# One subtraction per attention pass, from VectorE to GpSimd: the low half of expert 0's first weight

## The chip, the cores and the metric

The program runs on one core of a Trainium2 chip. The core has five engines with queues of their own, which meet at semaphores only: PE (TensorE, matmuls; PEld is its weight load), DVE (VectorE), ACT (ScalarE), POOL (GpSimd) and SP (SyncE, which here only issues DMA). The metric is the device time of one execution in microseconds (us).

## What is computed

Attention in two parts over 64 heads (8 batches of 8, 576 positions, 64 columns), added up, and then a mixture of 8 experts in which each of the 4608 tokens goes to one expert:

```python
q_d, k_d, v_d = means over groups of 4 positions      # "pooled"
out_up = np.repeat(sm_attn(q_d, k_d, v_d), 4, axis=2)
mask = np.abs(pos[:, None] - pos[None, :]) < 4        # local attention
out_local = softmax(where(mask, scale * q @ k.T, -1e9)) @ v
x = (out_up + out_local) as [4608, 512]
logits = x @ w_gate; expert_idx = argmax(logits)
for e in range(8):
    h = np.maximum(x_sorted[lo:hi] @ w1[e], 0.0)
    y_sorted[lo:hi] = h @ w2[e]
return gate_w[:, None] * y
```

All data are float32. A float32 product in the expert part is made of three matmuls on halves: each matrix is split into a high half (rounded to the type fp32r) and a low half (the difference), and high x high, high x low and low x high are added.

## The kernel before

**Passes.** The attention loop handles two heads at a time. `steps(i)` issues pass i, for i from 0 to 31, and the table `PASS` sets the order of everything in it. A pass works on several pairs at once: its entry `(f, a)` runs step f for pair i - a. What one engine does in a pass is issued to its queue in that order and runs in that order. Marks such as `"@w1"` are places where further work is put in with `at((pass, mark), ...)`.

**POOL in a pass.** In this order: `pool_v` (vdt, L216) for pair i; `pool_qk` (qkt, L205) for pair i + 1, which adds up the queries and keys in pairs; at the mark `@sc` none, one or two scatters, each of them a one-element memset of `spacer` (L470) and an indirect DMA of 128 rows from the buffer `xr` into the DRAM tensor `xs` (L471); `pool_qk2` (qkd, L211) for pair i + 1; `pool_v2` (vds, L222) for pair i. Of the passes spoken of here, 15, 17, 21, 23, 25 and 29 have two scatters, 18, 19, 22, 26, 27 and 30 have one, 16, 20, 24 and 28 have none.

**The other engines.** PE makes the scores on pooled data, `s_d` (L285, 12 matmuls), from qkd. DVE takes their maximum (mxd, L290), normalises (L274, L271), and in the next pass takes the maximum and sums of the local part (L249, L259), adds the result of an older pair into XT (L364, after ACT's outd, L354) and subtracts (L253). The bank pD that `s_d` writes is the only one, and comes free when ACT's three exponentials of the pair before (L299) and DVE's L271 are done. Passes 15, 19, 23 and 27 have a stage of the routing (`route_b`) on DVE and ACT; passes 16, 20, 24 and 28 have its last stage (`route_c`): among others DVE's L424 to L437 and ACT's L427 and L429. L429 and L437 write token numbers and gates into the rows of `xr` that earlier scatters read, and wait for these DMAs to have landed.

**The split of expert 0's first weight.** `split_w1` makes the halves w1h and w1l of a piece of the raw weight: ACT copies with rounding (L181), another engine subtracts (L182). For expert 0 it is called with `quarters`, one piece of 128x256 at the mark `@w1` of each of passes 15 to 30:

```python
    for j in range(4):
        for q in range(4):
            at((15 + j * 4 + q, "@w1"), split_w1, 0, j, (q,))
```

`@w1` stands behind `max_scale` (ACT, L293) and `norm` (DVE, L271) and ahead of `pool_qk2`, `exp_d` (ACT, L299) and `pool_v2`. For experts 1 to 7 it is called without `quarters`, in the expert part, on pieces of 128x512. The halves of expert 0 are first used behind the last pass.

Of the kernel before, what the change touches and what calls it, by code (L numbers as in the profile page):

```python
# [90 lines left out]
def attention_moe_kernel(ctx: ExitStack, tc: tile.TileContext, qk, vw, vd, wg, w1, w2, cst, csb, out):  # L91
    nc = tc.nc
# [80 lines left out]
    def split_w1(e, k, quarters=None, halves=(0, 1)):  # L173
        if (e, k) not in W1:
            pl = wpool if e % 2 == 0 else wodd[0]
            W1[e, k] = (pl.tile([128, F], F32R, name=f"w1h{k}"), pl.tile([128, F], F32R, name=f"w1l{k}"))
        hi, lo = W1[e, k]
        src = raws[place[1, e, k]]
        for s in [slice(a * 512, (a + 1) * 512) for a in halves] if quarters is None else [
                slice(a * 256, (a + 1) * 256) for a in quarters]:  # L180
            nc.scalar.activation(hi[:, s], src[:, s], AF.Copy)  # L181
            nc.vector.tensor_sub(lo[:, s], src[:, s], hi[:, s])  # L182

    outds = [p2.tile([128, QPAD // 2], F32, name=f"outd{i}", bufs=1) for i in range(2)]

# [602 lines left out]
# [3 lines that stand above are left out]
# [93 lines left out]
    for e in range(E):  # L884
        for f in range(8):
            if e > 0:
                s1(e, f)
                if f == 3:
                    rest = prep(e, 4, hold=True)
                if f == 4:  # L890
                    rest()
                split_w2(e, f)
                if f % 2 == 1:
                    raw_ahead(place[2, e, f // 2] + 6)
            else:
                s1(e, f, slice(EARLY.stop, FIRST))
            if e + 1 < E:
                if f == (0 if e == 0 else 4):
                    x_load(e + 1, 1)
                if f == 0 and e > 0:  # L900
                    x_load(e + 1, 0)
                if f == 4:
                    gi_load(e + 1, 0, 5)
                split_w1(e + 1, f // 2, halves=(f % 2,))
                if f % 2 == 1:
                    raw_ahead(place[1, e + 1, f // 2] + 6)
                if f == 6 and e + 2 < E:
                    pad_after(e + 2)
                if f == 7:
                    prep(e + 1, 0, 1)  # L910
                    gi_make(e + 1, 0, 5)
# [54 lines left out]
```

## Time and profile before

| | |
|---|---|
| median of 3 runs | 669.18 us (665.74 to 670.09) |
| the profiled execution's own time | 662.55 us |
| its span, first to last instruction | 660.6 us |
| PE busy | 625.5 us (95%) |
| DVE busy | 371.9 us (56%) |
| ACT busy | 320.0 us (48%) |
| POOL busy | 216.3 us (33%) |

A share of the whole span mixes three parts: the attention loop up to about 200 us, a stretch up to about 245 us in which the last tokens are routed, scattered and read back, and the experts, which are PE's. The passes that the change touches lie between 100 and 196 us; rows of that stretch are what is read below. In them an engine's row starts some hundredths of a microsecond before the row ahead of it has ended, so what an instruction takes out of its queue is read from start to start.

### The profile page before, as it was taken

How to read it: one execution, taken by the hardware profiler on the slowest of the kernel's cores; microseconds unless marked ns; L12 is line 12 of the kernel's file. 1: busy time of each engine (PE TensorE's matmuls, PEld its weight loads, DVE VectorE, ACT ScalarE, POOL GpSimd, SP SyncE). 2: the span in 40 equal slices, each digit the busy share in tenths (PEclk: the TensorE clock that was granted, in tenths of full speed). 3: DMA queues.
4: the chain of work that ended last, by engine and by line, in shares of the span. 5: the costliest groups of instructions: out<-in, count | busy, mean ns of one | idle time of the engine just before them, and what ended most of it. 6: DMA issues, size and time to landing. Idle time of an engine off the chain costs nothing.

```text
span 660.6 us, 15650 instructions
## 1 busy us (share of the span) xinstructions
PE 625.5 (95%) x6163; PEld 510.3 (77%) x6163; DVE 371.9 (56%) x691; ACT 320.0 (48%) x845; POOL 216.3 (33%) x316
## 2 busy tenths in 40 slices
PE   7988998999998989999999999999999989999994
PEld 3766776777776978888888888888888878888873
DVE  5968899999996646382373065166128247115020
ACT  3656777778785535362362254254236145224120
POOL 6955887888770611101101011101110101110111
PEclk9989999999999989999999999999999999999998
DMA  9999999899534496284176238238228528110001
GB/s 305 286 270 264 291 280 279 261 281 269 170 128 124 150 297 193 63 232 147 52 182 187 66 133 233 65 94 216 99 80 224 178 77 209 48 46 1 33 18 41
DMA packets 66226, 108.52 MB, mean 164 GB/s; under 512 B 15388, under 2 KB 36524, under 8 KB 66112
## 3 DMA queue, kind: packets, MB, share of 16 engines
q1 hardware_dynamic: 59840, 87.62, 47.8%
q0 software_dynamic: 5984, 19.01, 7.9%
q8 instruction: 66, 1.08, 0.7%
q10 hardware_dynamic: 288, 0.42, 0.2%
q14 instruction: 48, 0.39, 0.2%
HBM read 86.98 MB, written 23.67 MB: 167 GB/s over the span
## 4 chain that ended last, share of the span: by engine, by line
PE 68%; issue 10%; DVE 10%; DMA 4%; POOL 3%; ACT 2%; SPq 1%; POOLq 0%; another core or an unknown queue 0%; DVEq 0%; ACTq 0%
PE p L596 8%; PE p L597 8%; PE p L595 8%; PE p L611 7%; PE p L609 7%; PE p L610 7%; PE pD L285 3%; PE pPV L337 2%; PE pX L322 2%; PE pX L691 2%; PE pX L710 2%; DMA vd<-in_vd_dram 2%; PE pPV L350 1%; DVE A L271 1%; PE pS L236 1%
## 5 line engine op out<-in xcount | busy, mean ns | idle before, releaser
L595 PE MATMUL p<-xh,w1h 128*128 128x512 f32 (+1 forms) x288 | 106.7, 370 | 3.2 <-issue 1.9
L616 POOL DMA_INDIRECT out_dram<-y,tix x39 | 38.0, 974 | 212.9 <-ACT y L628 201.5
L596 PE MATMUL p<-xl,w1h 128*128 128x512 f32 (+1 forms) x288 | 106.0, 368 | 0.8 <-DVE xl L543 0.8
L597 PE MATMUL p<-xh,w1l 128*128 128x512 f32 (+1 forms) x288 | 105.9, 368 | 0.0
L609 PE MATMUL p<-w2h,hh 128*128 128x512 f32 x256 | 101.1, 395 | 0.0
L611 PE MATMUL p<-w2h,hl 128*128 128x512 f32 x256 | 99.8, 390 | 0.0
L610 PE MATMUL p<-w2l,hh 128*128 128x512 f32 x256 | 99.6, 389 | 0.0
L600 DVE SCALAR_TENSOR_TENSOR hl<-p,hh 128x512 fp32r<-128x512 f32 (+1 forms) x72 | 45.5, 632 | 93.3 <-ACT hh L599 91.3
L599 ACT ACTIVATE hh<-p 128x512 fp32r<-128x512 f32 (+1 forms) x72 | 39.6, 551 | 78.9 <-PE p L597 78.9
L628 ACT ACTIVATE y<-p,gi 128x512 f32<-128x512 f32 x32 | 22.0, 689 | 93.8 <-PE p L611 89.4
L595 PEld LDWEIGHTS p<-xh,w1h 128*128 128x128 f32 x288 | 55.0, 191 | 13.1 <-issue 2.3
L596 PEld LDWEIGHTS p<-xl,w1h 128*128 128x128 f32 x288 | 55.1, 191 | 9.7 <-DVE xl L543 0.9
L597 PEld LDWEIGHTS p<-xh,w1l 128*128 128x128 f32 x288 | 55.0, 191 | 8.7
L611 PEld LDWEIGHTS p<-w2h,hl 128*128 128x128 f32 x256 | 48.0, 188 | 10.2
L610 PEld LDWEIGHTS p<-w2l,hh 128*128 128x128 f32 x256 | 48.1, 188 | 9.6
L609 PEld LDWEIGHTS p<-w2h,hh 128*128 128x128 f32 x256 | 48.1, 188 | 9.4
L471 POOL DMA_INDIRECT xs<-xr,ix x36 | 36.8, 1021 | 42.0 <-ACT w1h L181 12.4
L182 DVE TENSOR_TENSOR w1l<-raw,w1h 128x512 fp32r<-128x512 f32 (+1 forms) x72 | 49.4, 686 | 0.8
L299 ACT ACTIVATE AD<-pD,mxd 128x144 f32<-128x144 f32 x96 | 35.3, 376 | 19.1 <-DVE A L271 18.8
L543 DVE TENSOR_TENSOR xl<-pX,xh 128x512 fp32r<-128x512 f32 x38 | 24.7, 684 | 35.2 <-ACT xh L542 34.2
L585 DVE TENSOR_TENSOR w2l<-raw,w2h 128x512 fp32r<-128x512 f32 x64 | 43.4, 681 | 1.1 <-ACT w2h L584 0.6
L216 POOL TENSOR_TENSOR vdt<-vd 72x512 f32<-72x512 f32 x32 | 40.8, 1276 | 6.4 <-DMA vd<-in_vd_dram 4.2
(148 smaller groups left out, 1204.7 us busy)
## 6 DMA issues: line engine op xcount, KB each, us to landing
raw<-in_w_dram SPq DMA_DIRECT2D x64, 512.0 KB
qk<-in_qk_dram SPq DMA_DIRECT2D x32, 583.0 KB
vw<-in_vw_dram SPq DMA_DIRECT2D x32, 320.0 KB
vd<-in_vd_dram SPq DMA_DIRECT2D x32, 288.0 KB
xrow<-xs SPq DMA_DIRECT2D x32, 192.0 KB
xrow<-xs SPq DMA_DIRECT2D x32, 128.0 KB
xs<-zs SPq DMA_DIRECT2D x6, 512.0 KB
xs<-pad SPq DMA_DIRECT2D x3, 257.0 KB
```

The costliest lines, as they stand in the source:

```text
L182: nc.vector.tensor_sub(lo[:, s], src[:, s], hi[:, s])
L216: nc.gpsimd.tensor_add(t2, v[:, 0:2], v[:, 2:4])
L585: nc.vector.tensor_sub(lo, src, hi)
L595: nc.tensor.matmul(p, wh[:, fs], xh[:, k, r], start=(k == 0), stop=False)
L596: nc.tensor.matmul(p, wh[:, fs], xl[:, k, r], start=False, stop=False)
L597: nc.tensor.matmul(p, wl[:, fs], xh[:, k, r], start=False, stop=(k == 3))
L599: nc.scalar.activation(hh[:, f, r], p, AF.Relu)
L600: nc.vector.scalar_tensor_tensor(hl[:, f, r], p, 0.0, hh[:, f, r], op0=OP.max, op1=OP.subtract)
L609: nc.tensor.matmul(p, hh, wh, start=(f == 0), stop=False)
L610: nc.tensor.matmul(p, hh, wl, start=False, stop=False)
L611: nc.tensor.matmul(p, hl, wh, start=False, stop=(f == 7))
L616: ins = nc.gpsimd.indirect_dma_start(out=out, out_offset=bass.IndirectOffsetOnAxis(ap=ix, axis=0), in_=y, in_offset=None, bounds_check=N - ...
```

## The change

One line: where `split_w1` is called with `quarters`, that is for expert 0 in the attention loop, the subtraction is issued on POOL instead of DVE. The other calls stay as they are.

```diff
@@ -179,7 +179,7 @@
         for s in [slice(a * 512, (a + 1) * 512) for a in halves] if quarters is None else [
                 slice(a * 256, (a + 1) * 256) for a in quarters]:
             nc.scalar.activation(hi[:, s], src[:, s], AF.Copy)
-            nc.vector.tensor_sub(lo[:, s], src[:, s], hi[:, s])
+            (nc.vector if quarters is None else nc.gpsimd).tensor_sub(lo[:, s], src[:, s], hi[:, s])
```

POOL's queue at passes 15 and 16, with the semaphores that each row waits for (Activation is ACT's, DMAHW and DMASW are DMA queues'); the first two rows are the end of pass 15's second scatter:

```order
 L470 MEMSET spacer 1x1 [waits Pool_49]
 L471 DMA xs<-xr,ix 42112x514 [waits DMASW1_49,Activation_49]
+L182 TENSOR_TENSOR w1l_2008<-raw,w1h_2007 128x256 [waits DMAHW0_49,Activation_49]
 L211 TENSOR_TENSOR qkd<-qkt 128x288 [waits PE_49]
 L222 TENSOR_TENSOR vds<-vdt 72x256
 L216 TENSOR_TENSOR vdt<-vd 72x512 [waits DMAHW0_49,Pool_49]
 L205 TENSOR_TENSOR qkt<-qk 128x576 [waits DMAHW7_49]
+L182 TENSOR_TENSOR w1l_2008<-raw,w1h_2007 128x256 [waits Activation_49]
 L211 TENSOR_TENSOR qkd<-qkt 128x288 [waits PE_49,Pool_49]
```

In each of the sixteen passes the subtraction stands behind the scatters and ahead of qkd, and waits for ACT. POOL's queue at pass 17, with two scatters:

```order
 L205 TENSOR_TENSOR qkt<-qk 128x576 [waits DMAHW2_49]
 L470 MEMSET spacer 1x1
-L471 DMA xs<-xr,ix 42112x514 [waits DMASW2_49,DVE_49,Activation_49]
+L471 DMA xs<-xr,ix 42112x514 [waits DMASW2_49,DVE_49]
 L470 MEMSET spacer 1x1 [waits Pool_49]
 L471 DMA xs<-xr,ix 42112x514 [waits DMASW3_49]
+L182 TENSOR_TENSOR w1l_2008<-raw,w1h_2007 128x256 [waits Activation_49]
 L211 TENSOR_TENSOR qkd<-qkt 128x288 [waits PE_49]
 L222 TENSOR_TENSOR vds<-vdt 72x256
@@ -108,5 +111,6 @@
```

The first scatter no longer waits for ACT itself, since the subtraction of pass 16 ahead of it in the queue has waited for a later instruction of ACT. DVE's queue at the turn from pass 15 to pass 16:

```order
 L274 TENSOR_TENSOR AD<-AD,pD 128x432
 L271 TENSOR_TENSOR A<-A,pD 128x640
-L182 TENSOR_TENSOR w1l_2008<-raw,w1h_2007 128x256
 L249 TENSOR_REDUCE mx<-pS 128x10
 L259 TENSOR_REDUCE smd<-A 128x10
```

Sixteen such rows go from DVE's queue; PE's and ACT's queues are the same row for row, with the same waits.

## Rows read from the trace of the kernel before

**Rows 1.** Two lines of the page's 40 slices (16.5 us each): DVE and POOL busy time in tenths.

```profile
DVE  5968899999996646382373065166128247115020
POOL 6955887888770611101101011101110101110111
```

**Rows 2.** Three stretches of four passes each (DVE's L249 of pass 16 to that of pass 20, then to 24, then to 28). Columns: length, then busy us and count of PE, PEld, DVE, ACT, POOL, then granted clock, DMA share, GB/s.

```profile
102.99:127.33 24.34, 22.76 (x519) 18.02 (x517) 22.96 (x49) 18.83 (x69) 20.43 (x26) 1.00 0.94 276
127.33:151.44 24.11, 22.39 (x511) 17.91 (x511) 23.51 (x49) 18.94 (x68) 19.30 (x25) 1.00 0.90 273
151.44:175.79 24.35, 22.79 (x521) 18.17 (x519) 23.00 (x50) 19.09 (x71) 21.05 (x27) 1.00 0.77 226
```

**Rows 3.** The only wait of DVE above 0.4 us at a time in passes 15 to 31 (99 to 200 us): us in total, times, longest.

```profile
DVE XT L364 <- ACT outd L354: 1.3, 2, 0.7
```

**Rows 4.** The subtraction on DVE: its group over the loop (busy us, mean ns), then one instance that ran freely with the POOL add beside it (pass 21), and one that did not (pass 22), with the DVE instruction behind it. Columns of the timeline rows: start us, us, engine, line.

```profile
L182 DVE TENSOR_TENSOR w1l<-raw,w1h 128x256 fp32r<-128x256 f32 x16 | 9.9, 616 | 0.0
138.42 0.42 DVE L182 TENSOR_TENSOR w1l<-raw,w1h 128x256 fp32r<-128x256 f32 x1
138.42 1.42 POOL L205 TENSOR_TENSOR qkt<-qk 128x576 f32<-128x576 f32 x1
143.73 1.14 POOL L205 TENSOR_TENSOR qkt<-qk 128x576 f32<-128x576 f32 x1
143.74 1.42 DVE L182 TENSOR_TENSOR w1l<-raw,w1h 128x256 fp32r<-128x256 f32 x1
145.08 0.81 DVE L249 TENSOR_REDUCE mx<-pS 128x10 f32<-128x640 f32 x1
```

**Rows 5.** What POOL waits for in passes 15 to 31: us in total, times, longest.

```profile
POOL xs L471 <- ACT w1h L181: 12.4, 4, 3.7
```

**Rows 6.** POOL in order of time, from the second step of pass 21's pooling to that of pass 24. The rows lie between 141.05 and 151.22 us.

```profile
141.05 0.67 POOL L211 TENSOR_TENSOR qkd<-qkt 128x288 f32<-128x288 f32 x1
141.68 0.72 POOL L222 TENSOR_TENSOR vds<-vdt 72x256 f32<-72x256 f32 x1
142.48 1.28 POOL L216 TENSOR_TENSOR vdt<-vd 72x512 f32<-72x512 f32 x1
...
144.82 0.09 POOL L470 MEMSET spacer<- 1x1 f32 x1
...
147.33 0.68 POOL L211 TENSOR_TENSOR qkd<-qkt 128x288 f32<-128x288 f32 x1
...
151.22 0.82 POOL L211 TENSOR_TENSOR qkd<-qkt 128x288 f32<-128x288 f32 x1
```

**Rows 7.** Two groups of POOL instructions: the longest two-input one of the loop, and the one of this shape with one input that writes the rounded type (from the expert part).

```profile
L216 POOL TENSOR_TENSOR vdt<-vd 72x512 f32<-72x512 f32 x16 | 20.5, 1282 | 1.3
L567 POOL CAST xb<-xh 128x256 fp32r<-128x256 f32 x8 | 3.2, 397 | 93.3 <-ACT xh L542 93.3
```

**Rows 8.** ACT's rounding copy w1h of passes 16, 20, 24 and 28, the passes without a scatter.

```profile
107.78 0.40 ACT L181 ACTIVATE w1h<-raw 128x256 fp32r<-128x256 f32 x1
...
132.15 0.40 ACT L181 ACTIVATE w1h<-raw 128x256 fp32r<-128x256 f32 x1
...
156.24 0.40 ACT L181 ACTIVATE w1h<-raw 128x256 fp32r<-128x256 f32 x1
...
180.60 0.40 ACT L181 ACTIVATE w1h<-raw 128x256 fp32r<-128x256 f32 x1
```

**Rows 9.** PE's scores on the pooled queries and keys (L285) of passes 18, 19, 30 and 31.

```profile
115.56 0.95 PE L285 MATMUL pD<-qkd 64*64 64x144 f32 x12
121.85 0.95 PE L285 MATMUL pD<-qkd 64*64 64x144 f32 x12
...
188.93 0.95 PE L285 MATMUL pD<-qkd 64*64 64x144 f32 x12
195.47 0.95 PE L285 MATMUL pD<-qkd 64*64 64x144 f32 x12
```

**Rows 10.** Pass 16: ACT's outd and DVE's add that waits for it. Pass 19: the subtraction on DVE and what follows it.

```profile
103.41 0.41 ACT L354 ACTIVATE outd<-pPV 128x288 f32<-128x288 f32 x1
104.45 0.75 DVE L364 TENSOR_TENSOR XT<-pPV,outd 128x580 f32<-128x580 f32 x1
...
126.64 0.77 DVE L182 TENSOR_TENSOR w1l<-raw,w1h 128x256 fp32r<-128x256 f32 x1
127.33 0.81 DVE L249 TENSOR_REDUCE mx<-pS 128x10 f32<-128x640 f32 x1
```

**Rows 11.** Median us from issue to landing of the scatters that were issued in 110 to 130, 130 to 160 and 160 to 200 us, and ACT's copy of token numbers in pass 20, which writes into the buffer the scatters read.

```profile
xs<-xr,ix POOLq DMA_INDIRECT x4, 8.0
xs<-xr,ix POOLq DMA_INDIRECT x7, 7.4
xs<-xr,ix POOLq DMA_INDIRECT x7, 3.5
131.96 0.18 ACT L429 COPY xr<-cf 128x5 f32<-128x5 f32 x1
```

## The prediction

> **What bounds the kernel now.** I read the 40 slices of the page first, to see which engine is full where the change acts. From slice 7 to 12, some 100 to 198 us, DVE stands at 9 tenths or more, and POOL at 7 or 8 [rows 1]. The table of stretches says the same in numbers: of each four passes, some 24.3 us, DVE is busy 23.0 to 23.5, PE 22.4 to 22.8 and POOL 19.3 to 21.1 [rows 2]. Then DVE's waits: in the sixteen passes there are only two of any size, 1.3 us together, for ACT's outd [rows 3]. So DVE sets the pace by a narrow margin over PE. An instruction that leaves DVE's queue is worth its time there, but only until PE, or whatever gets the instruction, is late.
>
> POOL's 20 of 24 us is work that runs ahead: it waits for ACT just four times in the loop, 12.4 us in all, each time at the first scatter behind a `route_c` [rows 5]. At all other places its queue holds only loads and its own adds, so that qkd is made most of a pass before PE wants it.
>
> **What the change takes from DVE.** Sixteen subtractions, 9.9 us in their group [rows 4]. A free one takes 0.42 us; the one of pass 22 takes 1.42, begun 0.01 us behind a POOL add of 1.14 us. Rows overlap their follower by 0.08 us (143.74 + 1.42 against 145.08), so what leaves the queue is 0.33 us for a free one and 9.9 - 16 x 0.08 = 8.6 us for all. That is the ceiling of the gain.
>
> The pairs in rows 4 show that the two engines take turns: in pass 21 the subtraction ran in 0.42 and the POOL add beside it took 1.42 instead of 1.14; in pass 22 it was the other way round. The Trainium skill has a rule for this (SBUF — State Buffer, section "SBUF: two separate sides"): a DVE instruction with two SBUF inputs and a GpSimd one take the shared port pair as an exclusive lock, and the later one stands still. The rows agree, and by it no large DVE instruction of the loop is left that could meet POOL; if POOL's adds met a lock in the new order too, each of the eight POOL adds of this kind on the path below would be 0.28 us longer, and the sum 2.2 us more.
>
> **What it adds to POOL.** One subtraction of 128x256 with two inputs per pass. No row shows it. The nearest are POOL's two-input adds: qkd with 288 elements, 0.67 us and 0.63 to the next start, and vds with 256 on fewer partitions, 0.72 us [rows 6]. I take 0.65 us of queue. The bounds: a one-input copy of this shape and output type takes 0.40 [rows 7], some 0.35 start to start; the longest two-input add, 512 elements, takes 1.28 [rows 7], some 1.24 start to start.
>
> The Trainium skill gives a figure for two-input elementwise work on this engine (GPSIMD Engine Reference, section "3.1 Elementwise — side-by-side cycle accounting"): 2.6 cycles an element. With its 1.2 GHz that is an estimate of 0.56 us for 256 elements without dispatch, and my sum would be 0.9 us smaller by it.
>
> **What it makes wait.** The new instruction waits for ACT's w1h of its pass, and behind it in POOL's queue stand qkd of the next pair, vds, vdt, qkt and the scatters. So POOL no longer runs ahead: who waits for it is PE, at `s_d` of the next pass. This is the step that decides. I follow the passes from one without a scatter, where POOL arrives early and waits for w1h, to the next.
>
> POOL's cycle from qkd to qkd, before: with no scatter 3.89 us (147.33 to 151.22), with two 6.28 (141.05 to 147.33), with one the mean of these, 5.08 [rows 6]. A signal costs 0.08 (vds ends at 142.40, vdt that waits for it starts at 142.48).
>
> From the end of w1h in pass 16 to `s_d` of pass 18: signal 0.08, subtraction 0.65, the cycle with pass 17's two scatters 6.28, subtraction 0.65, qkd 0.68, signal 0.08, together 8.42 us. Before it was 115.56 - 108.18 = 7.38 [rows 8, 9], with 0.33 of it DVE's. So there POOL is late by a microsecond. From `s_d` of pass 18 to that of pass 19 PE works without a gap on the routing matmuls, 6.29 us [rows 9], and the change does nothing. From there to the end of w1h in pass 20 it was 132.55 - 121.85 = 10.70 [rows 8, 9], of which 0.69 is DVE's subtraction of pass 19 (126.64 to 127.33) [rows 10]: 10.01. Sum 24.72 against 24.37: **0.35 lost** in four passes, though DVE got rid of its subtractions.
>
> A second wait hangs on the scatters, which also get later. L429 and L437 of pass 20 wait until the scatter of pass 19 has landed, and L429 starts 0.59 us ahead of the end of w1h (131.96 to 132.55) [rows 8, 11]. In the new order that scatter starts at 0.08 + 0.65 + 6.28 + 0.65 (qkd of pass 18), + 5.08 + 0.65 (qkd of 19), + 3.77 (vds, vdt, qkt; 141.05 to 144.82), + 0.09 (memset) = 17.25 us after pass 16's w1h. Landing took 8.0 us in the median there [rows 11]; with 0.59 behind it the end of w1h is at 25.84, **1.5 later** than before instead of 0.35. In passes 20 to 24 the same path with a landing of 7.4 us gives 25.24 against 156.64 - 132.55 = 24.09: **1.15 later**. Behind 160 us a scatter lands in 3.5 us and this wait is gone: passes 24 to 28 lose 0.35. Passes 28 to 30 lose 8.42 - (188.93 - 181.00) = 0.5, and from there PE works to pass 31 in 6.54 us as before [rows 8, 9].
>
> At the start there is a gain: pass 15's subtraction is gone, and in pass 16 DVE's add into XT (104.45) can come forward to the end of ACT's outd (103.82), **0.6 earlier** [rows 10].
>
> **The sum:** -0.6 + 1.5 + 1.15 + 0.35 + 0.5 = **2.9 us slower**. Ten subtractions lie on this path (three to pass 20, three to 24, two to 28, two to 30), so between the bounds of 0.35 and 1.24 us for one it is -0.1 to +8.8. If the landings do not bind it is +1.0. Behind the loop everything starts from the end of the last passes, the experts are PE's, and I let the shift through as it is. Nothing there uses w1l sooner: POOL's last subtraction ends some 10 us before the experts begin.
>
> Against the profiled execution's own 662.55 us that is 665.5. The median of the runs is 669.18, and I put the forecast on it: 672.1, a change of 0.4%.
>
> **The rivals.** *POOL is not late.* If qkd is ready whenever PE wants it, the stretch to `s_d` of pass 18 is 7.38 - 0.33 = 7.05, and four passes take 7.05 + 6.29 + 10.01 = 23.35, 1.0 less. Three times that, 0.6 at the start and 0.3 in the last passes: -3.9 us, 658.6, or 665.3 on the median. For it speaks that POOL was idle 12.4 us in the loop; against it, that this idle time lies in the four passes without a scatter and can't be moved to those with two. The ceiling of 8.6 us would need PE to have slack, and it has none behind the routing matmuls.
>
> *The subtraction on POOL is as long as vdt.* Same place, `s_d` behind the passes with two scatters; at 1.24 us in place of 0.65 the loss is 8.8 us, 671.4 or 678.0. It decides for slower by over 1% from 0.65 + (6.7 - 2.9) / 10 = 1.03 us. For it: 512 elements on 72 partitions cost 1.28, more than qkt with 576 [rows 4, 7], so elements alone don't set POOL's time. Against it: both adds near this size lie at 0.67 and 0.72.
>
> That the instruction is not moved at all is excluded by the order of the queues.
>
> **How the numbers follow.** The forecast with its two forms (landings bind or not) gets 0.72, POOL not late 0.12, a gain near the ceiling 0.03, a subtraction of 1 us and more 0.13. About 1% is what a measurement of this kernel tells from no change. Within it lie the forecast and most of the first rival: 0.83; faster by more 0.04, slower by more 0.13. The range reaches from just under the first rival, 664, to just over the second, 679.
>
> **What would show it.** In the profile of the changed kernel the subtraction stands on POOL, sixteen times, 0.65 to 0.75 us. POOL's waits for w1h move to the subtraction of passes 16, 20, 24 and 28. PE waits for qkd at `s_d` of passes 18, 22, 26 and 30, and DVE, full before, shows waits of some microseconds. The ends of w1h in those four passes are 24.7 us or more apart, 25 and more where L429 or L437 waits for a landing. I am wrong if DVE stays without waits, if PE's `s_d` never waits for POOL, or if the subtraction takes a time far from 0.65.

## The result, and the profile after

In one series of alternating runs the changed kernel took 672.66 us (median of 20) and the kernel before 666.13 us (20): a ratio of 1.0086, 95% interval 1.0066 to 1.0106. The ratios leave out executions over 1.5% above the fastest of their kernel, here three of the changed one. A later series gave 1.0040 (1.0009 to 1.0071). The change makes the kernel slower by 0.4 to 0.9%. The profiled execution of the changed kernel takes 671.53 us, its span is 669.5 us.

DVE is no longer full. The two lines of the page's slices that answer to [rows 1]:

```profile
DVE  5968889889885547274274056157128238115020
POOL 6955777899890610101101101111110101110111
```

The same three stretches as in [rows 2], from L249 of pass 16 to that of pass 20, 24 and 28 (length, then busy us and count of PE, PEld, DVE, ACT, POOL, clock, DMA share, GB/s):

```profile
102.79:127.75 24.96, 22.73 (x530) 18.10 (x523) 21.78 (x45) 18.71 (x68) 21.73 (x29) 1.00 0.84 257
127.75:152.34 24.59, 22.43 (x512) 17.96 (x512) 21.81 (x46) 19.06 (x69) 21.73 (x30) 1.00 0.81 263
152.34:177.50 25.16, 22.65 (x530) 18.08 (x523) 21.91 (x45) 18.60 (x68) 22.79 (x30) 1.00 0.75 234
```

DVE works 1.1 to 1.7 us less per four passes, POOL 1.3 to 2.4 us more, and each four passes last 0.5 to 0.8 us longer. No engine is full in them now, so the time went into waits between engines. DVE's, PE's and POOL's waits in 99.6 to 204.1 us (total, times, longest), to be set against [rows 3] and [rows 5]:

```profile
DVE mx L249 <- PE pS L236: 3.8, 4, 1.0
DVE XT L364 <- ACT outd L354: 3.8, 17, 0.9
...
PE pD L285 <- POOL qkd L211: 3.4, 4, 1.2
...
POOL w1l L182 <- ACT w1h L181: 10.2, 7, 3.4
```

POOL's wait for w1h has moved from the scatters to the subtraction, DVE waits for PE, and PE waits for POOL's qkd. Two groups of POOL in the same stretch, the subtraction and the add that stood beside it on DVE in [rows 4]:

```profile
L205 POOL TENSOR_TENSOR qkt<-qk 128x576 f32<-128x576 f32 x15 | 17.2, 1144 | 0.0
...
L182 POOL TENSOR_TENSOR w1l<-raw,w1h 128x256 fp32r<-128x256 f32 x16 | 11.8, 736 | 10.4 <-ACT w1h L181 10.2
```

POOL in order of time from pass 16, without a scatter, to the middle of pass 17, with two (the answer to [rows 6]):

```profile
108.32 0.73 POOL L182 TENSOR_TENSOR w1l<-raw,w1h 128x256 fp32r<-128x256 f32 x1 [1.57 <-ACT w1h L181]
109.01 0.67 POOL L211 TENSOR_TENSOR qkd<-qkt 128x288 f32<-128x288 f32 x1
...
115.26 0.75 POOL L182 TENSOR_TENSOR w1l<-raw,w1h 128x256 fp32r<-128x256 f32 x1
115.95 0.68 POOL L211 TENSOR_TENSOR qkd<-qkt 128x288 f32<-128x288 f32 x1
```

The subtraction of pass 16 waits, all that follows starts late, and qkd at 115.95 ends just when PE takes it. ACT's w1h of passes 16, 20, 24 and 28 (the answer to [rows 8]) and PE's `s_d` of passes 18, 22 and 30 (to [rows 9]; the square bracket is the idle time ahead of a row):

```profile
107.84 0.40 ACT L181 ACTIVATE w1h<-raw 128x256 fp32r<-128x256 f32 x1
132.84 0.40 ACT L181 ACTIVATE w1h<-raw 128x256 fp32r<-128x256 f32 x1
157.60 0.40 ACT L181 ACTIVATE w1h<-raw 128x256 fp32r<-128x256 f32 x1
182.59 0.40 ACT L181 ACTIVATE w1h<-raw 128x256 fp32r<-128x256 f32 x1
...
116.68 0.95 PE L285 MATMUL pD<-qkd 64*64 64x144 f32 x12 [0.80 <-ACT smd L262]
...
141.68 0.95 PE L285 MATMUL pD<-qkd 64*64 64x144 f32 x12 [0.71 <-POOL qkd L211]
...
191.43 0.95 PE L285 MATMUL pD<-qkd 64*64 64x144 f32 x12 [0.45 <-POOL qkd L211]
```

The ends of w1h are 25.00, 24.76 and 24.99 us apart, against 24.37, 24.09 and 24.36 before. The scatter of pass 19 and the ACT copy of pass 20 that needs it landed, with the median landing of the scatters of 99.6 to 204 us, answer to [rows 11]:

```profile
125.62 0.98 POOL L471 DMA_INDIRECT xs<-xr,ix  x1 [0.16 <-issue]
...
132.53 0.21 ACT L427 ACTIVATE gt<-gt 128x5 f32<-128x5 f32 x1 [0.16 <-DVE gt L426]
132.65 0.18 ACT L429 COPY xr<-cf 128x5 f32<-128x5 f32 x1
```

```profile
xs<-xr,ix POOLq DMA_INDIRECT x18, 5.6
```

L429 follows L427 without a gap: it waited for no landing.

**Behind the loop**, where the prediction let the shift through unchanged, the larger part was lost. The turn into the last stretch in the kernel before: pass 31's scatters, `s_d` of pass 31, the read-back `xrow` that waits for these scatters (L507), its first use on DVE (L538), PE's transposes of the next pair (L309), and the last add into XT.

```profile
193.42 0.96 POOL L471 DMA_INDIRECT xs<-xr,ix  x1 [0.21 <-issue]
195.47 0.95 PE L285 MATMUL pD<-qkd 64*64 64x144 f32 x12
196.60 2.16 SPq L507 DMA_DIRECT2D xrow<-xs  x4
203.94 1.32 DVE L538 STREAM_TRANSPOSE p<-xrow 128x512 f32<-128x512 f32 x2
206.50 0.55 PE L309 MATMUL pX<-cf,A 128*128 128x128 f32 x3 [1.68 <-ACT AT L316]
210.44 0.76 DVE L364 TENSOR_TENSOR XT<-pPV,outd 128x580 f32<-128x580 f32 x1 [0.97 <-ACT outd L354]
```

The same in the changed kernel:

```profile
200.55 0.96 POOL L471 DMA_INDIRECT xs<-xr,ix  x1 [0.21 <-issue]
203.65 1.82 SPq L507 DMA_DIRECT2D xrow<-xs  x4
208.25 1.32 DVE L538 STREAM_TRANSPOSE p<-xrow 128x512 f32<-128x512 f32 x2 [1.82 <-DMA xrow<-xs]
209.06 1.14 ACT L542 ACTIVATE xh<-p 128x512 fp32r<-128x512 f32 x2 [2.33 <-POOL spacer L470]
210.81 0.90 PE L309 MATMUL pX<-cf,A 128*128 128x128 f32 x3 [3.51 <-ACT AT L316]
217.04 0.76 DVE L364 TENSOR_TENSOR XT<-pPV,outd 128x580 f32<-128x580 f32 x1 [1.79 <-ACT outd L354]
```

and, in the columns of the stretches above, the ten microseconds in which PE comes back:

```profile
210.00:220.00 10.00, 8.50 (x118) 7.28 (x119) 4.03 (x14) 3.15 (x11) 0.00 (x0) 0.70 0.23 86
```

POOL comes out of the loop late (`s_d` of pass 31 is at 197.94 us here). Its last scatter starts 2.61 us behind `s_d` of pass 31 instead of 2.05 us ahead of it, and `xrow` is read 5.71 us behind it instead of 1.13. DVE's transpose waits 1.82 us for that data; ACT's copy of the transposed rows (L542) waits for the transpose, although its bracket names POOL, and behind it in ACT's queue stand the copies AT (L316) that PE's L309 waits for; and PE is idle for 3.51 us in one piece instead of 1.68. After that PE comes back slowly: three matmuls of L309 take 0.90 us instead of 0.55, and the granted clock of 210 to 220 us is 0.70 (a mix of 1.2 and 2.4 GHz; it is 0.50 from 210 to 216 us), where the kernel before has 1.00 from 204 to 214 us. From `s_d` of pass 31 to the last add into XT it is 19.10 us instead of 14.97, a loss of 4.13.

The loop from `s_d` of pass 15 to that of pass 31, before and after, in the columns of the stretches:

```profile
97.56:195.47 97.91, 91.33 (x2066) 72.88 (x2065) 93.90 (x194) 76.75 (x276) 80.71 (x101) 1.00 0.79 237
98.20:197.94 99.74, 90.94 (x2065) 72.84 (x2064) 87.80 (x178) 75.88 (x276) 85.33 (x112) 1.00 0.73 229
```

So of the 8.9 us between the spans 0.64 were there before the first subtraction (`s_d` of pass 15 at 98.20 instead of 97.56), 1.83 are the loop's, 4.13 the turn's, and 2.3 lie between the last add into XT and the end of the span; these I can't attribute from one execution each.

### The profile page after: what moved, and what is told of

Read it like the earlier page. It is cut to its first block, busy times and chain, and to the rows that moved or that the text cites. A ratio compares the mean times of both kernels' runs of the same rounds, so it can differ in the third digit from the quotient of the medians.

```text
span 669.5 us, 15638 instructions
## 1 busy us (share of the span) xinstructions
PE 628.8 (94%) x6160; PEld 513.6 (77%) x6163; DVE 365.7 (55%) x675; ACT 319.1 (48%) x845; POOL 224.6 (34%) x332
## 4 chain that ended last, share of the span: by engine, by line
PE 65%; issue 10%; POOL 9%; DVE 6%; DMA 5%; ACT 3%; SPq 1%; POOLq 0%; another core or an unknown queue 0%; DVEq 0%; ACTq 0%
PE p L596 8%; PE p L595 8%; PE p L597 8%; PE p L609 7%; PE p L611 7%; PE p L610 7%; POOL xs L471 2%; PE pD L285 2%; POOL vdt L216 2%; POOL qkt L205 2%; PE pX L691 2%; PE pX L710 2%; ACT AD L299 2%; DMA xs<-xr,ix 1%; DMA vd<-in_vd_dram 1%
## 5 line engine op out<-in xcount | busy, mean ns | idle before, releaser
L610 PE MATMUL p<-w2l,hh 128*128 128x512 f32 x256 | 99.6, 389 | 0.0
L285 PE MATMUL pD<-qkd 64*64 64x144 f32 x384 | 31.2, 295 | 13.9 <-POOL qkd L211 6.8
L299 ACT ACTIVATE AD<-pD,mxd 128x144 f32<-128x144 f32 x96 | 35.3, 376 | 17.5 <-DVE A L271 17.4
```

The lines of the kernel that those rows point to most:

```text
L285: nc.tensor.matmul(p[h * 64:h * 64 + 64, j * SD:(j + 1) * SD], qf[r, j * DB:j * DB + 64], x[r, 1, :], start=True, stop=True)
L299: nc.scalar.activation(AD[i][:, j], PD[i][:, j * SD:(j + 1) * SD], AF.Exp, scale=SCD, bias=MXD[i][:, j:j + 1], accum_out=SMD[i][:, NG + j: ...
L610: nc.tensor.matmul(p, hh, wl, start=False, stop=False)
```

## The experiments

Theory A, after this trace: the cost is the chain "wait for w1h, then POOL's queue", in the loop and in pass 31's scatters behind it; take the wait away and POOL has room for the subtraction. Theory B: POOL is short of time, wherever the subtraction stands. Theory C, in the expectations: only the late scatters of pass 31 cost. The runs were made in three series on three chips, on which the kernel before takes 677.57, 676.40 and 677.74 us; ratios are to the runs of the kernel before in the same series. Columns four to six are read from one profiled execution each: the distances of the ends of w1h from pass 16 to 20, 24 and 28, and the time from `s_d` of pass 31 to the last add into XT, called the end of the loop below.

| series, kernel | median, us | ratio (95%) | four passes, us | end of loop, us |
|---|---|---|---|---|
| 1 e1_two_later | 671.63 | 0.9901 (0.9865 to 0.9937) | 24.20, 24.21, 24.51 | 15.9 |
| 1 e2_no_low | 676.20 | 0.9976 (0.9951 to 1.0000) | 25.07, 25.63, 24.62 | 17.4 |
| 1 e3_wait_alone | 676.99 | 0.9985 (0.9960 to 1.0011) | 25.41, 25.37, 25.12 | 17.3 |
| 1 e4_last_on_dve | 679.20 | 1.0025 (0.9999 to 1.0051) | 27.21, 26.14, 26.54 | 15.0 |
| 2 r0_before | 676.16 | one execution | 25.72, 26.77, 25.71 | 15.0 |
| 2 r1_after | 678.63 | 1.0040 (1.0009 to 1.0071) | 25.98, 25.99, 25.92 | 17.8 |
| 2 e5_late_scatter | 678.31 | 1.0031 (1.0004 to 1.0059) | 25.73, 26.76, 25.72 | 19.8 |
| 2 e6_no_low_dve | 674.07 | 0.9966 (0.9935 to 0.9996) | 24.70, 25.58, 24.32 | 15.0 |
| 3 e7_twice | 688.68 | 1.0156 (1.0125 to 1.0187) | 27.81, 28.05, 28.25 | 18.9 |
| 3 e8_one_later | 672.98 | 0.9917 (0.9894 to 0.9941) | 24.22, 24.26, 24.42 | 16.0 |
| 3 e9_dve_two_later | 679.67 | 1.0010 (0.9988 to 1.0032) | 25.66, 27.55, 26.44 | 15.3 |
| 3 e10_two_later_again | 672.99 | 0.9910 (0.9883 to 0.9938) | 24.21, 24.22, 24.48 | 15.8 |

**The two kernels again.** In the trace of the second series the kernel before is itself 1.4 to 2.7 us slower per four passes than in its first trace.

> The kernel before, for its trace on the chip of these runs. If this chip is like the first, the ends of w1h in passes 16, 20, 24, 28 lie 24.4, 24.1 and 24.4 us apart and PE shows no wait marked as issue in the loop's second half; if PE's own issue gaps lengthen the loop here, as in the traces of the four experiments before (e2_no_low: three gaps of 0.4 us ahead of one matmul group alone), this trace has them too and the distances are over 24.5.

> The changed kernel beside the others on one chip. By the first measurement 1.007 to 1.011 times the kernel before. If its loss hangs on a chip on which DMA and PE's issue are quick, the ratio is nearer to 1 here. In its trace the stretch from the last scores (pass 31) to the last add into XT is 19 us, of which 4 are the wait for the rows of expert 0.

r1_after loses again, and its turn behind the loop is 2.8 us longer than that of r0_before: the transpose waits 0.83 us for `xrow`, and PE is idle for 2.52 us ahead of L309. Its loop is not longer, though: from `s_d` of pass 15 to that of pass 31 it takes 104.74 us, r0_before 105.64, and in its rows no `s_d` waits for qkd. That the loop loses is seen in the first pair of traces only. r0_before has the gaps that its expectation names (1.5 us in the loop marked issue, that is without a cause in the profile) and distances over 24.5.

**The subtraction later (e1, e8, e9, e10).** ACT's copy stays where it is; POOL subtracts in a later pass, so that w1h is ready long before. `split_w1` has two new arguments for it, which part to issue ("h" is ACT's copy, "l" the subtraction) and the subtraction's engine `eng`; the diffs from here on show the lines that matter and leave out the rest.

```diff
-            at((15 + j * 4 + q, "@w1"), split_w1, 0, j, (q,))
+            at((15 + j * 4 + q, "@w1"), split_w1, 0, j, (q,), (0, 1), "h")
+            at((17 + j * 4 + q, "@w1"), split_w1, 0, j, (q,), (0, 1), "l", nc.gpsimd)
```

> ACT's rounding copy stays in passes 15 to 30, POOL's subtraction of each piece is issued two passes later, in passes 17 to 32, at the same mark. POOL does the same work but its subtraction no longer waits for ACT. Theory A (the wait for w1h takes POOL's lead away, and that is what costs): POOL runs ahead again, the ends of w1h in passes 16, 20, 24, 28 lie 23.3 to 24.3 us apart (24.4, 24.1, 24.4 before; 25.0, 24.8, 25.0 in the changed kernel), PE waits for qkd under 2 us in the loop, and the time is 0 to 4 us under the kernel before. Theory B (POOL's time is what costs, sixteen times 0.69 us in a full queue): the distances stay at 24.7 or more, and the time stays 3 to 6 us over the kernel before. Theory C (only the late scatters of pass 31 cost): the distances don't matter, the first read of scattered rows behind the loop starts within 1 us of where it did before relative to the last scores, and the time is that of the kernel before within 2 us.

> As e1_two_later (the subtraction on POOL, issued in a later pass than its ACT copy), but one pass later instead of two. If the cost of the change is POOL's wait for ACT in a pass without a scatter, one pass of lead already takes it away, and this is as fast as e1_two_later: a ratio to the kernel before of 0.990, within 0.004. If it is POOL's time, both are alike too, but both would have been slower than before, which e1_two_later was not. If two passes are needed (POOL runs ahead of ACT by more than a pass), this lies between: 0.995 to 1.004, with POOL waits for w1h left in the profile.

> The kernel before, with the subtraction left on DVE but issued two passes after its ACT copy, as in e1_two_later. It tells whether e1_two_later gains from POOL or from the place. DVE is full, so by the reading that the gain is DVE's relief this is as the kernel before: 1.000, within 0.003. If the gain comes from the place (DVE or its followers waited for w1h), it is 0.990 to 0.996.

> e1_two_later once more, beside the other two: POOL subtracts two passes after the ACT copy. 0.990 again, within 0.004, if that gain is the kernel's and not of one series of runs; PE's waits marked issue in the loop stay below 2 us in the profile if their lack explains that it beat the kernels without any subtraction.

e8 has 16 for 17; e9 has DVE for POOL. With POOL the kernel is 0.8 to 1.0% faster than before, in three runs on two chips; with DVE, two passes later too, nothing is gained (1.001). So the gain comes with the engine and not with the place alone, and one pass of lead is as good as two (in e8's trace one subtraction still waits, for 1.5 us). e1's gain is larger than theory A allowed (5.9 us in the medians, for 0 to 4), and its third distance, 24.51, lies outside 23.3 to 24.3. POOL's waits in e1 and two of its rows, 105 to 205 us:

```profile
POOL xs L473 <- issue: 10.2, 15, 4.7
...
124.38 0.73 POOL L184 TENSOR_TENSOR w1l<-raw,w1h 128x256 fp32r<-128x256 f32 x1
125.07 0.67 POOL L213 TENSOR_TENSOR qkd<-qkt 128x288 f32<-128x288 f32 x1
```

The subtraction takes the same 0.73 us and waits for nothing; no PE row of e1 in the loop waits for POOL. Theory B falls: POOL's work is the same as in the changed kernel. So does theory C, by which e1 would have been within 2 us of the kernel before. e10's expectation on PE's waits marked issue was not met: between 99 and 205 us they are 1.6 us at `s_d`, 0.7 at L339 and 0.9 elsewhere, 3.2 instead of under 2.

How much of the gain is DVE's relief is not shown. The loops of r0_before and e10, from `s_d` of pass 15 to that of pass 31:

```profile
101.67:207.31 105.64, 95.39 (x2066) 73.60 (x2065) 96.08 (x194) 76.73 (x277) 79.92 (x100) 1.00 0.71 218
103.86:202.72 98.86, 91.71 (x2065) 72.86 (x2064) 87.65 (x177) 75.84 (x274) 86.57 (x114) 1.00 0.75 230
```

e1 and e8 take 98.76 and 98.84 us. That is 7 us less than r0_before, but no less than the 97.91 of the kernel before in its first trace. r0_before's PE is busy 4 us longer with as many matmuls, at the same granted clock, for a cause that the profile doesn't show; e9's loop (106.70 us) has this too, and a granted clock of 0.50 from 157 to 163 us. So the later subtraction removes PE's wait for POOL, but what it would gain where the kernel before runs as in its first trace was not measured.

**No subtraction, or almost none (e2, e3, e6).** e2 and e6 leave the low half out (zeros are written ahead of the loop, by POOL in e2 and DVE in e6); e3 lets POOL subtract 2 of the 256 columns, behind the same wait (its line, against e1's `split_w1`):

```diff
-                (eng or nc.vector).tensor_sub(lo[:, s], src[:, s], hi[:, s])
+                t = s if quarters is None else slice(s.start, s.start + 2)
+                (eng or nc.vector).tensor_sub(lo[:, t], src[:, t], hi[:, t])
```

> No engine subtracts in the loop: the low half of expert 0's first weight is left out and is zero (filled before the loop). It is the most that DVE's relief can be worth. By the first rival of the prediction: 3.9 us under the kernel before, with the ends of w1h in passes 16, 20, 24, 28 some 23.35 us apart, because PE has no slack behind the routing matmuls. If DVE alone set the pace: 8.6 us under it.

> POOL subtracts 2 of each 256 columns, at the same place and with the same wait for w1h; the rest of the low half is left out and is zero. Same wait as in the changed kernel, an instruction of some 0.15 to 0.2 us instead of 0.73. If the wait alone costs (the strongest form of theory A), the ends of w1h stay 24.5 us or more apart and PE still waits for qkd in passes 18, 22, 26, 30. By the sum of the prediction the path from w1h to the scores two passes later is 8.42 - 2 x 0.5 = 7.4 us, as long as it was before (7.38), so the distances are 23.7 to 23.9 and the time 2 to 4 us under the kernel before. By theory B it is that of the kernel without a subtraction within 1 us.

> As e2_no_low (no subtraction of expert 0's low half, which is zero), but the zeros are written by DVE ahead of the loop and not by POOL, whose fill held up the first pooling by 2.6 us in e2_no_low. If only that fill separated e2_no_low (0.998) from e1_two_later (0.990), this run is at 0.988 to 0.992 of the kernel before, some 6 to 8 us under it. If it stays at 0.996 or more, the relief of DVE itself is worth little, because PE takes over (its rival in the prediction: -3.9 us, 0.994).

In the medians the wait by itself costs nothing that can be seen (e3 as e2, each known to some 0.25%), so the strong form of theory A, by which the wait is the whole cost, falls too: it needs POOL's time behind it. The expectations were missed otherwise: e3's distances are over 25 where 23.7 to 23.9 was forecast, its time 0.6 us under the kernel before and not 2 to 4, and its pass 31 is late for `xrow` all the same (the transpose waits 0.40 us, PE 2.09). e2's end of 17.4 us comes without a late read: PE waits 1.68 us there as before, and the granted clock falls to 0.50 behind it. And to be rid of the subtraction altogether is worth 0.2 to 0.3% only, where 3.9 us (0.6%) was forecast for e2, and less than e1's 1.0% with the same relief of DVE; e6, without e2's fill on POOL, is no better. Where e6 lost is in its trace: from `s_d` of pass 15 to that of pass 31 it takes 103.43 us, e10 98.86; in four passes, each with routing matmuls on PE, it is longer (18 to 19: 7.15 against 6.29; 22 to 23: 7.20 against 6.09; 26 to 27: 6.75 against 6.30; 30 to 31: 10.03 against 7.32), and these four make 5.1 us. The last of them in e6, PE's rows, and the stretch behind them:

```profile
200.50 0.30 PE L243 MATMUL pS<-qk 64*58 64x64 f32 x3 [0.38 <-issue]
201.22 0.33 PE L243 MATMUL pS<-qk 64*58 64x64 f32 x4 [0.41 <-issue]
201.94 0.26 PE L243 MATMUL pS<-qk 64*58 64x64 f32 x1 [0.40 <-issue]
```

```profile
204.00:206.00 2.00, 2.00 (x15) 1.96 (x10) 1.38 (x2) 1.01 (x2) 0.00 (x0) 0.50 0.73 164
```

In the midst of a run of equal matmuls PE stands still, for a cause that the profile doesn't show, and then runs at half its clock. Gaps of this kind, at the scores (L243 here) and at L344, come to 2.5 us in e6 between 99 and 205 us and to 0.7 in e10 at the same operations; but r1_after has 3.7 and r0_before 0.4. So they show where this execution of e6 lost against e10; whether they are why e1 beats e6 in the medians, and what brings them about, stays open.

**The slope (e7).** Each subtraction is issued twice on POOL.

```diff
             (nc.vector if quarters is None else nc.gpsimd).tensor_sub(lo[:, s], src[:, s], hi[:, s])
+            if quarters is not None:
+                nc.gpsimd.tensor_sub(lo[:, s], src[:, s], hi[:, s])
```

> After, with each of the sixteen subtractions issued twice on POOL, back to back (the second writes the same values again). It measures what a subtraction on the path costs. By the prediction's path (ten subtractions between the ends of w1h of passes 16 and 30, 0.69 us each from start to start) it is 6.9 us above the changed kernel, +1.0% of ratio over it, and the ends of w1h in four passes lie 1.4 to 2.1 us further apart than in the changed kernel. If POOL has slack again after the first subtraction (the path lies elsewhere), it stays within 2 us of the changed kernel.

```profile
115.09 0.73 POOL L182 TENSOR_TENSOR w1l<-raw,w1h 128x256 fp32r<-128x256 f32 x1 [0.76 <-ACT w1h L181]
115.90 0.73 POOL L184 TENSOR_TENSOR w1l<-raw,w1h 128x256 fp32r<-128x256 f32 x1
116.59 0.67 POOL L213 TENSOR_TENSOR qkd<-qkt 128x288 f32<-128x288 f32 x1
```

Two that write the same place are 0.81 us apart, and the distances of the ends of w1h grow by 1.8 to 2.3 us over r1_after's (forecast 1.4 to 2.1). `s_d` of pass 18 is 10.07 us behind the end of w1h of pass 16 (125.08 - 115.01), 1.63 more than in the changed kernel: twice 0.81. The ratio is 1.0116 times that of r1_after, some 7.8 us; the ten of the prediction's path make 8.1. Without landings that bind, which is how it came out below, only eight lie on it (two per four passes, two to pass 30), and they make 6.5. From e3, whose subtraction takes 0.19 us, to r1_after it is 0.55%, 3.7 us, for 0.54 us more per subtraction, which is seven. These are ratios of different series, known to 0.3% or so, and seven, eight and ten can't be told apart by that. They agree with the prediction's path, of which the 10.07 us show one stretch directly.

**The turn behind the loop (e4, e5).** e4 is the changed kernel with the last four subtractions (passes 27 to 30) on DVE, so that POOL leaves the loop as before. e5 is the kernel before with four extra adds on POOL ahead of pass 31's scatters.

```diff
-            at((15 + j * 4 + q, "@w1"), split_w1, 0, j, (q,))
+            at((15 + j * 4 + q, "@w1"), split_w1, 0, j, (q,), (0, 1), "hl", nc.gpsimd if j < 3 else nc.vector)
```

```diff
+    def busy(n):
+        for _ in range(n):
+            nc.gpsimd.tensor_add(junk, VD[31][:, 0:2], VD[31][:, 2:4])
+    at((31, "@x"), busy, 4)
```

> The subtractions of passes 15 to 26 on POOL, those of 27 to 30 on DVE as before the change. In the changed kernel the scatters of pass 31 start 4.7 us later against the last scores than before, SP's first read of scattered rows waits for them, PE idles 3.5 us behind it and comes back at half its clock. If the tail costs what is missing in the prediction's sum (theory C and my account): POOL has its lead again by pass 31, the tail loss of some 4 us is gone, the loop's loss is that of two groups and a half less, and the time is 0 to 2 us over the kernel before. If the tail hangs on something else: 4 us or more over it.

> The kernel before, with four more adds of 72x512 on POOL (some 5 us) ahead of the two scatters of pass 31, and nothing else. If the tail loss comes from the late scatters alone, SP's first read of scattered rows starts some 5 us later, PE idles 3 us or more behind it and the time is 3 to 4.5 us over the kernel before (1.0045 to 1.007). If what is late in the tail of the changed kernel is something else (the low half itself, the last vds), the time is the same within 1 us.

e4's transpose has no wait:

```profile
220.91 1.32 DVE L540 STREAM_TRANSPOSE p<-xrow 128x512 f32<-128x512 f32 x2
```

and e5 reproduces the turn of the changed kernel, DVE's wait and PE's idle time and half clock with it:

```profile
215.13 1.32 DVE L538 STREAM_TRANSPOSE p<-xrow 128x512 f32<-128x512 f32 x2 [1.88 <-DMA xrow<-xs]
217.70 0.90 PE L309 MATMUL pX<-cf,A 128*128 128x128 f32 x3 [3.57 <-ACT AT L316]
```

The end of the loop is 15.0 us in e4, as before, and 19.8 in e5, so late scatters of pass 31 are shown to be the cause of the longer turn. (The four adds hold back the vds of pass 31 as well, but no PE row of e5's turn waits for it.) What it is worth in the median is less: e5 costs 0.31%, 2.1 us, though its turn is 4.8 longer in the profile and 3 to 4.5 was forecast. e4 as a whole (1.0025, 1.6 us over the kernel before, within its forecast) can't be told from the changed kernel of the other series (1.0040); its four passes take 26.1 to 27.2 us, with a granted clock of 0.50 from 124 to 127 us.

## Why the prediction was right, and where not

It said 672.1 us, 0.4% slower, and within 1%. The direction is right and "within 1%" held: +0.86% in the first series, twice the forecast, and +0.40% in a later one. That 672.1 lies next to the 672.66 measured is luck: it stands on a median of three runs, 669.18, and twenty gave 666.13, so the change measured there is 6.5 us and not 2.9. Errors of opposite sign hide in the sum, too: it has 1.95 us of landings that did not come, and lacks 0.9 us in the loop and 4.1 behind it.

*Right, to a few hundredths.* The subtraction on POOL: 0.74 us, 0.69 to the next start, where 0.65 was taken. The Trainium skill's 2.6 cycles an element (GPSIMD Engine Reference, section "3.1 Elementwise — side-by-side cycle accounting"), by which the estimate was 0.56 us without dispatch, lies below the measured row; the rows of POOL's neighbours were the better guide. From the end of w1h of pass 16 to `s_d` of pass 18: 8.42 forecast, 8.44 measured (108.24 to 116.68). `s_d` of pass 18 to that of 19: 6.29 and 6.29. The start: -0.6 and -0.58 (from `s_d` of pass 15 to the end of w1h of pass 16, 10.62 before and 10.04 after). Passes 28 to 31: +0.5 and +0.48. The scatter of pass 19: 17.25 us behind w1h of pass 16 and 17.38. The waits stand where they were named, PE's at passes 22, 26 and 30, at 24 too, and at 18, where the bracket names ACT's smd, though POOL's qkd ended only 0.05 us ahead of PE (115.95 + 0.68).

*The exclusive lock.* With no subtraction on DVE, POOL's qkt is 1.14 us long in the mean of 15 (1.23 before), so the 2.2 us for locks in a new order did not come. This agrees with the Trainium skill (SBUF — State Buffer, section "SBUF: two separate sides"), by which a DVE instruction with two SBUF inputs and a GpSimd one lock each other out: with this one gone from DVE, POOL's qkt shows no lock.

*Mis-sized: four passes.* +0.35 forecast without a landing, +0.63, +0.67 and +0.63 measured. The step that failed is "10.70 less DVE's 0.69" from `s_d` of pass 19 to w1h of pass 20: it took 10.27 and not 10.01. DVE came forward by its subtraction (L249 of pass 20 is 4.78 us behind that `s_d`, which is at 122.97, instead of 5.48), but ACT's outd, which it needs soon after, did not (6.05 us behind that `s_d`, 6.04 before). outd of pass 20 before, then outd and the add behind it after:

```profile
127.89 0.42 ACT L354 ACTIVATE outd<-pPV 128x288 f32<-128x288 f32 x1
...
129.02 0.41 ACT L354 ACTIVATE outd<-pPV 128x288 f32<-128x288 f32 x1
129.46 0.76 DVE L364 TENSOR_TENSOR XT<-pPV,outd 128x580 f32<-128x580 f32 x1 [0.16 <-ACT outd L354]
```

DVE lost 0.25 us of its lead there: the add starts 6.49 us behind that `s_d` instead of 6.94. In the loop it waits seventeen times for outd, where it had waited twice [rows 3].

*Wrong: the landings.* +1.15 and +0.8 of the sum stood on scatters that would land too late for L429. The scatter started when I said, but L429 of pass 20 began 7.03 us later without a wait for it, where I had taken 8.0 for the landing. The median I used was that of the kernel before, whose DMA share in that stretch is 0.94 [rows 2]; in the changed kernel it is 0.84, and the median landing of the loop is 5.6 us (7.0 before). A landing measured on one schedule is no constant of the next.

*Wrong: "I let the shift through as it is".* I followed POOL's lateness to the last `s_d`, which wants qkd, and not to POOL's last scatters, which want nothing of PE but hold back the read of `xs`. The turn lost 4.13 us by it in the first pair of traces, 2.8 in the second, and e5's late scatters alone cost 2.1 us in the median. The loop by itself was forecast at +1.0 without landings and lost 1.83.

*The rivals.* "POOL is not late" was given -3.9 us. It is not what the change does; but e1, e8 and e10 make its condition true and gain more, 0.8 to 1.0% (5.6 to 6.7 us), below the ceiling of 8.6. Its mechanism is not confirmed by that: four passes take 24.2 to 24.5 us there and not 23.35, and the gain stands against a kernel before whose loop is longer than the one that the rival was worked out on. Against it I had argued that POOL's idle time in the passes without a scatter can't be moved to those with two. That was wrong: with a subtraction that does not wait POOL runs ahead, and no PE row of e1 waits for it. "As long as vdt" is refuted by the 0.74; e7, which puts 1.5 us in its place, agrees with the slope of that rival within its error.

## What to carry to other kernels

An instruction that is moved to an engine with idle time can take that engine's lead away if it brings a wait with it and enough work behind the wait: look at whether the producer of its operands is ahead of the new engine's queue, and if it isn't, issue the consumer one stage later; here PE then no longer waited for POOL, and a loss of 0.4 to 0.9% became a gain of 0.8 to 1.0%, of which the runs leave open how much is DVE's relief. Follow the lateness to the last instruction of the queue, not only to the first one that waits for it: the most expensive waiter in both pairs of traces was a read behind the loop. Compare a gain with the trace of the kernel before from the same series: its loop took 97.9 us in one and 105.6 in another. Do not carry a DMA latency from one schedule to another as if it were fixed.

## What the runs showed of the hardware

After 3.51 us without a matmul PE came back at half its clock (0.50 granted from 210 to 216 us); e5 repeats it with 3.57 us, and behind 2.52 us in r1_after and 2.09 in e3 the same three matmuls took 0.90 us instead of 0.55 too. After 1.68 us they took 0.55 in before, r0_before, e4 and e2; in e2 the granted clock fell to 0.50 within a microsecond all the same. PE showed gaps that the profile marks as issue, up to 0.4 us each in the midst of equal matmuls, in the three later series, in which the kernel before takes 676 to 678 us; in e6 three of them in a row were followed by 2 us at a granted clock of 0.50. In the first traces of before and after there is none in the loop. The kernel before also ran its four passes in 25.7 to 26.8 us instead of 24.1 to 24.4 in the second of these series (r0_before; e5 too, which is the same kernel up to pass 31), for reasons that the runs don't show. Two POOL instructions that write the same place start 0.81 us apart, where different ones start 0.69 apart.
